# Set-up of a fused FFT and expert layer on one core: unit sums, weight pieces and the order of the early parts

## The chip, the core and the metric

The kernel runs on one NeuronCore of a Trainium2 chip. The core has five engines with queues of their own, each strictly in order: TensorE (PE, its weight loads as PEld), VectorE (DVE), ScalarE (ACT), GpSimd (POOL) and SyncE (SP), which here only starts DMA transfers. TensorE writes to PSUM, the others work in SBUF; GpSimd does not reach PSUM. The metric is the time of one execution on the device in microseconds (us); lower is better.

## The reference

For each of 8 batches a sequence of 3072 rows of 256 numbers goes through a two-dimensional Fourier transform, of which the real part stays. Every one of the 24576 rows then goes through one expert layer of width 2048.

```python
X = np.fft.fft(x, axis=1)            # x: 8 x 3072 x 256
X = np.fft.fft(X, axis=2)
t = X.real.astype(np.float32).reshape(8 * 3072, 256)
h = t @ w_in                         # w_in: 256 x 2048, float64 as given
sp = np.where(h > 20.0, h, np.log1p(np.exp(np.minimum(h, 20.0))))
g = h * np.tanh(sp)                  # the Mish function
out = (g @ w_out).astype(np.float32) # w_out: 2048 x 256, float64 as given
```

## The kernel before

**The transform is folded into the layer.** The second transform is multiplied into w_in once, which gives a cosine and a sine matrix `wch` and `wsh`, each with a rest `wcl` and `wsl` (every fp32 number is held as a rounded part and a rest, so that TensorE's faster fp32r form can be used three times for one exact product). The first transform is a fold (sums and differences of rows on DVE and POOL) followed by matmuls with a table `dft`. A batch gives three chunks of 1024 output rows, held as 512 columns.

**Steps.** The main loop runs over 384 steps: 8 batches x 3 chunks x 16 slices f of the hidden width. Step tau does, in this order: `mm1(tau)`, six matmuls of 512 columns into two PSUM tiles `pa` and `pb` (two buffers of each); `mm2(tau-6)`, twelve matmuls into four accumulators; `make_h(tau)`, three DVE operations from PSUM into a place of the ring `hring`; `split(tau-4)`, in which ACT rounds that step's values to `gh` and POOL computes the rest `gl`; ACT's Mish on the new place; and then whatever is due in the set-up or in the fold of the next batch. `gh` and `gl` have two buffers each, and `hring` has RH = 9 places of 1024 columns, so that make_h(tau) takes the place of step tau-9.

**Set-up.** The weights arrive as float64 bit patterns, in pieces: eight of w_in (two make one quarter of the matrices, which serves four slices f) and eight of w_out (each serves two slices). `load_w` fetches a piece, `conv` turns it into fp32 in three parts: part 0 two DVE bit operations, part 1 two ACT operations, part 2 two DVE operations and a multiply, which is on DVE or POOL as its last argument says (L526). `make_wc` does the matmuls of a quarter, `make_wl` (DVE, L555 and L556) its rests, `split_out` rounds a piece of w_out on ACT (L561) and computes its rest `wol` on POOL (L562). For batch 0, `add_n1` sums the three parts of a unit of x with an identity matrix on TensorE (L676), `fold_z` folds the sums, and `chunk0` gives the first chunk; the sums of the other two chunks follow in `pairs0` and `sums0`, half on DVE (tiles e), half on POOL (tiles o). `other_chunks` makes chunk 1 from them. `col_z`, `col_cs` and `col_out` make the rows of column 0, in 8 partitions.

**What sets the order.** The schedule is written by hand. The table EARLY names a step, a part and its arguments; -1 is before the loop, and within a step the parts are issued in the table's order. OTHER0_AT holds the steps of other_chunks for batch 0, FOLD_AT the steps at which the fold of the next batch begins. `room` says where a piece of weights lives: the first four pieces of w_in in the ring `hring`, the first of w_out in the buffers of gh and gl, the rest in the places of x.

Of the kernel before, what the change touches and what calls it, by code (L numbers as in the profile page):

```python
# [132 lines left out]
OTHER0_AT = (6, 7, 8, 10)  # L133

XPLACES = [('out', 1), ('in', 4), ('in', 5), ('out', 2), ('out', 3), ('in', 6), ('in', 7), ('out', 4), ('out', 5), ('out', 6), ('out', 7)]
EARLY = [
    (-1, 'make_mids', ()),
# [23 lines left out]
    (0, 'conv', ('in', 2, 0)),  # L161
    (0, 'conv', ('in', 3, 0)),
    (0, 'conv', ('in', 2, 1)),
    (0, 'conv', ('in', 3, 1)),
    (0, 'pairs0', (0,)),
    (1, 'conv', ('in', 2, 2, "V")),
    (1, 'conv', ('in', 3, 2, "V")),
    (1, 'sums0', (0, 0, 3)),
    (2, 'make_wc', (1, 0)),
    (2, 'sums0', (0, 3, 7)),  # L170
    (2, 'conv', ('out', 0, 0)),
    (2, 'conv', ('out', 0, 1)),
    (2, 'make_wl', (1,)),
# [4 lines left out]
    (2, 'load_w', ('in', 5)),
    (2, 'load_w', ('out', 2)),
    (3, 'conv', ('out', 0, 2, "V")),  # L180
    (3, 'split_out', (0,)),
    (3, 'sums0', (1, 0, 3)),
    (3, 'col_z', (0,)),
    (3, 'col_z', (1,)),
    (4, 'sums0', (1, 3, 7)),
    (4, 'put_mids', ()),
    (4, 'col_cs', (0,)),
    (4, 'conv', ('in', 4, 0)),
# [3 lines left out]
    (5, 'col_cs', (1,)),
    (5, 'conv', ('in', 4, 2, "V")),
    (5, 'conv', ('in', 5, 2, "V")),
    (5, 'conv', ('out', 1, 0)),
    (5, 'conv', ('out', 1, 1)),
# [704 lines left out]
```

## Time and profile before

| | |
|---|---|
| median of 3 runs (lowest to highest) | 1792.13 us (1790.42 to 1794.56) |
| the profiled execution, its own time | 1792.64 us |
| its span, first to last instruction | 1790.9 us |
| mean granted TensorE clock | 0.984 of full speed |
| busy over the span: PE, PEld | 1738.2 us (97%), 1415.2 us (79%) |
| busy over the span: DVE, ACT, POOL | 1091.0 us (61%), 866.1 us (48%), 1158.5 us (65%) |

Times in rows are microseconds from the span's first instruction. The profile's page gives the whole span in 40 slices of some 45 us: TensorE's busy share is 6, 6, 8 and 8 tenths in the first four of them and 9 from the fifth on. So the rows below look at the first 210 us, and at a few places later for comparison.

### The profile page before, as it was taken

What the parts mean: (1) busy time and instruction counts of PE and PEld (TensorE: products, weight loads), DVE (VectorE), ACT (ScalarE), POOL (GpSimd) and SP (SyncE); (2) the same over time, 40 slices, a digit from 0 to 9 for tenths busy, and PEclk for the clock granted to TensorE, in tenths of its full rate; (3) what the DMA queues carried; (4) which work ended last, traced back from release to release, by engine and by line L of the source; (5) the groups of instructions that cost most, each with busy time, mean ns of one, the idle gap of its engine ahead of it and who ended that gap; (6) DMA issues with size and microseconds to landing.
All of it is one profiled execution on the core that took longest, in us unless ns stands there. A gap on an engine that the chain in (4) does not pass through costs nothing.

```text
span 1790.9 us, 20402 instructions
## 1 busy us (share of the span) xinstructions
PE 1738.2 (97%) x7564; PEld 1415.2 (79%) x7564; DVE 1091.0 (61%) x1635; ACT 866.1 (48%) x968; POOL 1158.5 (65%) x618
## 2 busy tenths in 40 slices
PE   6688899999999999999999999999999999999999
PEld 3356688888888888888888888888888888888887
DVE  3996676556655656556655666556565566554453
ACT  1354454455544545445544555445454555444454
POOL 0536686577765877568765777568765787555455
PEclk8799999999999999999999999999999999998999
DMA  4111200200002000110002000020002000000000
GB/s 164 48 55 52 82 1 30 101 1 30 30 1 100 30 0 30 57 44 30 30 1 100 8 23 30 1 100 30 0 30 100 1 30 30 1 30 1 30 24 24
DMA packets 25158, 67.70 MB, mean 38 GB/s; under 512 B 3043, under 2 KB 3402, under 8 KB 24930
## 3 DMA queue, kind: packets, MB, share of 16 engines
q1 hardware_dynamic: 24354, 64.86, 9.9%
q10 hardware_dynamic: 704, 1.54, 0.2%
q8 instruction: 59, 0.97, 0.2%
q14 instruction: 41, 0.34, 0.1%
HBM read 41.14 MB, written 25.25 MB: 37 GB/s over the span
## 4 chain that ended last, share of the span: by engine, by line
PE 93%; DVE 4%; DMA 1%; POOL 1%; ACT 0%; issue 0%; SPq 0%; DVEq 0%; ACTq 0%
PE acc L755 58%; PE pa L725 5%; PE pa L726 5%; PE pa L727 5%; PE pb L725 5%; PE pb L727 5%; PE pb L726 5%; PE pa L390 2%; PE pb L390 2%; POOL gl L745 0%; DVE woutu L524 0%; DVE hring L735 0%; DVE hring L736 0%; DMA xring<-x_dram 0%; PE pu L676 0%
## 5 line engine op out<-in xcount | busy, mean ns | idle before, releaser
L745 POOL TENSOR_TENSOR gl<-hring,gh 128x1024 fp32r<-128x1024 f32 x384 | 927.2, 2415 | 537.5 <-ACT gh L744 523.9
L744 ACT CAST gh<-hring 128x1024 fp32r<-128x1024 f32 x384 | 403.2, 1050 | 762.5 <-PE acc L755 758.0
L755 PE MATMUL acc<-gh,wol 128*128 128x512 f32 x1536 | 600.5, 391 | 7.8 <-POOL wol L562 7.8
L755 PE MATMUL acc<-gh,woh 128*128 128x512 f32 x1536 | 600.3, 391 | 4.1 <-ACT woh L561 4.1
L734 DVE SCALAR_TENSOR_TENSOR hring<-p0b,wc,pa 128x512 f32<-128x512 f32 x384 | 286.7, 747 | 475.3 <-PE pa L727 455.2
L755 PE MATMUL acc<-gl,woh 128*128 128x512 f32 x1536 | 424.6, 391 | 0.0
L843 ACT ACTIVATE hring<-hring 128x1024 f32<-128x1024 f32 x384 | 404.2, 1053 | 25.1 <-DVE hring L736 25.1
L755 PEld LDWEIGHTS acc<-gh,wol 128*128 128x128 f32 x1536 | 289.6, 189 | 69.4 <-POOL wol L562 9.0
L755 PEld LDWEIGHTS acc<-gh,woh 128*128 128x128 f32 x1536 | 289.4, 188 | 66.0 <-ACT woh L561 5.8
L755 PEld LDWEIGHTS acc<-gl,woh 128*128 128x128 f32 x1536 | 290.2, 189 | 60.7
L735 DVE TENSOR_TENSOR hring<-hring,pb 128x512 f32<-128x512 f32 x384 | 264.0, 688 | 41.7 <-DVE hring L734 1.4
L736 DVE TENSOR_TENSOR hring<-hring,pb 128x512 f32<-128x512 f32 x384 | 263.8, 687 | 13.3
L725 PE MATMUL pa<-ph,wch 128*128 128x512 f32 x384 | 160.2, 417 | 4.3 <-ACT pe L610 3.3
L725 PE MATMUL pb<-qh,wsh 128*128 128x512 f32 x384 | 150.5, 392 | 0.9 <-DVE hring L736 0.9
L726 PE MATMUL pa<-pl,wch 128*128 128x512 f32 x384 | 150.6, 392 | 0.3 <-DVE pl L406 0.3
L727 PE MATMUL pa<-ph,wcl 128*128 128x512 f32 x384 | 150.4, 392 | 0.0
L727 PE MATMUL pb<-qh,wsl 128*128 128x512 f32 x384 | 150.0, 391 | 0.0
L726 PE MATMUL pb<-ql,wsh 128*128 128x512 f32 x384 | 149.9, 390 | 0.0
L725 PEld LDWEIGHTS pa<-ph,wch 128*128 128x128 f32 x384 | 72.8, 190 | 21.3 <-ACT pe L610 3.8
L315 POOL TENSOR_TENSOR o<-xring 128x768 f32<-128x768 f32 x32 | 59.8, 1872 | 44.0 <-DVE F1o L688 43.9
L725 PEld LDWEIGHTS pb<-qh,wsh 128*128 128x128 f32 x384 | 72.6, 189 | 17.0 <-DVE hring L736 1.8
L727 PEld LDWEIGHTS pa<-ph,wcl 128*128 128x128 f32 x384 | 72.6, 189 | 15.5
(205 smaller groups left out, 1125.4 us busy)
## 6 DMA issues: line engine op xcount, KB each, us to landing
xring<-x_dram SPq DMA_DIRECT2D x32, 768.0 KB
out_dram<-ot SPq DMA_DIRECT2D x96, 256.0 KB
p0b<-p_d SPq DMA_DIRECT2D x23, 256.0 KB
xring<-w_out_dram SPq DMA_DIRECT2D x7, 512.0 KB
hring<-w_in_dram SPq DMA_DIRECT2D x4, 512.0 KB
xring<-w_in_dram SPq DMA_DIRECT2D x4, 512.0 KB
dft<-table_dft_dram ACTq DMA_DIRECT2D x1, 1028.0 KB
wraw<-w_out_dram SPq DMA_DIRECT2D x1, 512.0 KB
```

Of the source, the lines that this page charges most:

```text
L315: eng.tensor_tensor(st[c, y, 0][:, w], r[:, :, 0], r[:, :, 1], op=ALU.add if y == "e" else ALU.subtract)
L390: T.matmul(dst, lhs(c), const(c, par, sine), **{"start": c == 0, "stop": c == last, **kw})
L725: T.matmul(dst, wh[:, fs], q[n + "h"], start=True, stop=False)
L726: T.matmul(dst, wh[:, fs], q[n + "l"], start=False, stop=False)
L727: T.matmul(dst, wl[:, fs], q[n + "h"], start=False, stop=True)
L734: V.scalar_tensor_tensor(h[:, 0:512], p0b[ch], wc0[:, f:f + 1], pa, op0=ALU.mult, op1=ALU.add)
L735: V.tensor_tensor(h[:, 512:1024], h[:, 0:512], pb, op=ALU.add)
L736: V.tensor_tensor(h[:, 0:512], h[:, 0:512], pb, op=ALU.subtract)
L744: A.copy(gh, h)
L745: G.tensor_tensor(gl, h, gh, op=ALU.subtract)
L755: T.matmul(acc[i], w[:, f, 128 * d:128 * d + 128], g[:, 512 * t:512 * t + 512], **kw)
L843: A.activation(hring[:, tau % RH], hring[:, tau % RH], AF.Mish)
```

## The change

The diff, cut to the code and to two lines of the table. The new table has 94 rows before its tail where the old one had 91; what its order does is shown below the diff.

```diff
-RH = 9
-FOLD_AT = (20, 10, 44)
+RH = 6
+FOLD_AT = (16, 10, 44)
-OTHER0_AT = (6, 7, 8, 10)
+OTHER0_AT = (11, 12, 13, 14)
-XPLACES = [('out', 1), ('in', 4), ('in', 5), ('out', 2), ('out', 3), ...]
+WPLACES = [('in', 0), ('in', 1), ('out', 0), ('out', 1), ('in', 4), ('in', 5), ('out', 2), ('in', 6), ('in', 7)] + [
+    ('out', i) for i in range(3, NF // 2)]
 EARLY = [
+    (-1, 'warm', (3,)),
...
+    (10, 'sums0', (1, 0, 3)),
...
 ] + [(t, g, a) for i in range(4, NF // 2) for t, g, a in (
-    (2 * i + 4, 'conv', ('out', i, 0)),
-    (2 * i + 4, 'conv', ('out', i, 1)),
-    (2 * i + 5, 'conv', ('out', i, 2, "V")),
-    (2 * i + 5, 'split_out', (i,)),
-)]
+    (2 * i + 3, 'conv', ('out', i, 0)),
+    (2 * i + 3, 'conv', ('out', i, 1)),
+    (2 * i + 4, 'conv', ('out', i, 2)),
+    (2 * i + 4, 'split_out', (i,)),
+    (2 * i + 4, 'load_w', ('out', i + 2)),
+)[:5 if i + 2 < NF // 2 else 4]]
...
+    wring = cp.tile([128, 2, 6 * D], F32, name="wring")
...
     def room(kind, i):
-        if kind == "in" and i < 4:
-            q, k = divmod(i, 2)
-            r = [hring[:, 4 * q + j] for j in range(4)]
-            return r[k], r[2][:, 512 * k:512 * k + 512], r[3][:, 512 * k:512 * k + 512]
-        if kind == "out" and i == 0:
+        if kind == "in" and i in (2, 3):
             tu = gp.tile([128, 1024], F32, tag="gl", name="wtu")
             return gp.tile([128, 1024], F32, tag="gh", name="wraw"), tu[:, :512], tu[:, 512:]
-        r = xring[:, XPLACES.index((kind, i)) % 4]
-        return r[:, :1024], r[:, 1024:], otp.tile([128, 512], F32, tag="ot", name="woutu")
+        r = wring[:, WPLACES.index((kind, i)) % 2]
+        return r[:, :1024], r[:, 1024:], otp.tile([128, 512], F32, tag="ot", name="wu")
...
-    load_w("out", 0)
...
-    def add_n1(c, w):
+    def add_n1(c, w, eng):
         u = 2 * c + w
-        pu = ps(("pa", "pb")[w]) if c == 0 else psacc.tile([128, 512], F32, tag=f"acc{2 + w}", name="pu")
...
+        x = [xring[:, u, 512 * n1:512 * n1 + 512] for n1 in range(3)]
+        if eng == "T":
+            pu = ps(("pa", "pb")[w])
...
+        else:
+            t = fp.tile([128, 512], F32, tag="full1", name="sum")
+            V.tensor_tensor(t, x[0], x[1], op=ALU.add)
+            V.tensor_tensor(t, t, x[2], op=ALU.add)
+            V.tensor_tensor(su, t[:, 0:256], t[:, 256:512], op=ALU.add)
+            V.tensor_tensor(sv, t[:, 0:256], t[:, 256:512], op=ALU.subtract)
+
+    zero = fp.tile([128, 512], F32, tag="full0", name="zero")
+    G.memset(zero, 0.0)
+
+    def warm(n):
+        pz = psacc.tile([128, 512], F32, tag="acc3", name="warm")
+        for _ in range(n):
+            T.matmul(pz, zero[:, :128], zero, start=True, stop=True)
...
-    def pairs0(c):
-        for w in range(2):
-            for y, eng in (("e", V), ("o", G)):
-                pair(0, c, w, y, eng)
+    def pairs0(c, w):
+        for y, eng in (("e", V), ("o", G)):
+            pair(0, c, w, y, eng)
```

With the old table every conv of part 2 in the diff and in the kernel names "V", DVE; in the new one only the first four pieces of w_in do, and the other twelve multiplies are on POOL. The parts pairs0 and sums0 stood in steps 0 to 4 and stand in steps 5 to 10 now; split_out of a w_out piece stands two steps ahead of the first mm2 that uses it, where it stood one step ahead.

TensorE before the loop, in the kernel before (`pw` are the matmuls of w_in's first quarter, `p_213` the first chunk's row):

```order
L576 MATMUL pb<-mids,hring 24x128
L577 MATMUL pb<-mids,hring 1x128
L584 MATMUL pc<-hring,mids 128x16
L585 MATMUL pc<-hring,mids 128x8
L676 MATMUL pa<-xring,hring 128x512 x3
L543 MATMUL pw<-hring,cs 128x512 x4
L676 MATMUL pb<-xring,hring 128x512 x3
L550 MATMUL pw<-ones,hring 128x1 x8
L676 MATMUL pu<-xring,hring 128x512 x3
L639 MATMUL p_213<-dft,hring 128x256 x4
```

The same stretch of TensorE now (three more matmuls on `zero` stand at the very start of the queue):

```order
L578 MATMUL pb<-mids,hring 24x128
L579 MATMUL pb<-mids,hring 1x128
L586 MATMUL pc<-hring,mids 128x16
L587 MATMUL pc<-hring,mids 128x8
L699 MATMUL warm<-zero 128x512 x3
L680 MATMUL pa<-xring,hring 128x512 x3
L680 MATMUL pb<-xring,hring 128x512 x3
L545 MATMUL pw<-wring,cs 128x512 x4
L552 MATMUL pw<-ones,wring 128x1 x8
L641 MATMUL p_224<-dft,hring 128x256 x4
```

The sums of two units stand together, ahead of the first quarter's matmuls, and those of the other two units have left TensorE.

POOL from the split of step 0 to that of step 3, in the kernel before (`wol` is the rest of a w_out piece, `o` and `F1o` are POOL's half of the fold):

```order
L745 TENSOR_TENSOR gl<-hring,gh 128x1024
L325 TENSOR_SCALAR o<-o 128x2x128
L326 TENSOR_TENSOR o<-o 128x2x128
L335 TENSOR_TENSOR o<-o 128x2x128
L344 TENSOR_TENSOR F1o<-o 128x256 x2
L745 TENSOR_TENSOR gl<-hring,gh 128x1024 x2
L562 TENSOR_TENSOR wol<-xring,woh 128x512
L406 TENSOR_TENSOR pl<-spare,ph 128x256
L745 TENSOR_TENSOR gl<-hring,gh 128x1024
```

POOL from the split of step 4 to that of step 6 now (L528 is the multiply of a piece of weights, L321 the pairs):

```order
L762 TENSOR_TENSOR gl<-hring,gh 128x1024
L564 TENSOR_TENSOR wol<-wring,woh 128x512
L331 TENSOR_SCALAR o<-o 128x2x128
L332 TENSOR_TENSOR o<-o 128x2x128
L341 TENSOR_TENSOR o<-o 128x2x128
L350 TENSOR_TENSOR F0o<-o 128x256 x2
L762 TENSOR_TENSOR gl<-hring,gh 128x1024
L528 TENSOR_TENSOR wring<-wring,wu 128x512
L321 TENSOR_TENSOR o<-xring 128x768
L528 TENSOR_TENSOR wring<-wring,wu 128x512
L762 TENSOR_TENSOR gl<-hring,gh 128x1024
```

Before, the first half of the fold was done before the first split and the second half ended right behind it; now both halves stand between the splits of steps 1 to 7, together with the multiplies.

POOL around the splits of steps 12 to 14 now, where the last two pieces of w_out and the next batch's first pair fall:

```order
L762 TENSOR_TENSOR gl<-hring,gh 128x1024 x2
L528 TENSOR_TENSOR wring<-wring,wu 128x512
L564 TENSOR_TENSOR wol<-wring,woh 128x512
L762 TENSOR_TENSOR gl<-hring,gh 128x1024
L412 TENSOR_TENSOR pl<-full_779,ph 128x512
L321 TENSOR_TENSOR o<-xring 128x768
L762 TENSOR_TENSOR gl<-hring,gh 128x1024
L528 TENSOR_TENSOR wring<-wring,wu 128x512
L564 TENSOR_TENSOR wol<-wring,woh 128x512
L412 TENSOR_TENSOR ql<-full_780,qh 128x512
```

Each `wol` has its multiply right ahead of it on the same queue now, and the pair L321 has come in front of the last piece.

## Rows read from the trace of the kernel before

**Rows 1.** Windows: busy time (instructions) of each engine by stage; granted clock, DMA.

```profile
0.00:46.45 46.45, 32.00 (x89) 16.64 (x89) 16.92 (x49) 8.80 (x21) 2.30 (x6) 0.89 0.40 158
46.45:138.49 92.04, 69.93 (x260) 43.44 (x259) 82.89 (x126) 39.44 (x63) 40.50 (x32) 0.87 0.19 67
138.49:205.50 67.01, 55.13 (x208) 42.73 (x207) 42.06 (x58) 30.64 (x39) 38.55 (x21) 0.90 0.17 59
205.50:1790.90 1585.40, 1581.15 (x7014) 1312.43 (x7012) 949.09 (x1405) 787.23 (x846) 1077.15 (x563) 1.00 0.09 32
```

**Rows 2.** Timeline, TensorE before the loop: start, duration, operation, [idle before it, releaser].

```profile
11.78 4.45 PE L676 MATMUL pa<-xring,hring 128*128 128x512 f32 x6 [3.56 <-DMA xring<-x_dram]
...
19.58 6.61 PE L543 MATMUL pw<-hring,cs 128*128 128x512 f32 x8 [3.35 <-issue]
...
43.26 0.70 PE L390 MATMUL pa<-dft,F1e 128*128 128x258 f32 x2 [1.17 <-DVE F1e L688]
...
46.45 0.50 PE L725 MATMUL pa<-ph,wch 128*128 128x512 f32 x1
```

**Rows 3.** Timeline, DVE: the first piece's part 2 behind the first unit's sum.

```profile
17.47 0.68 DVE L524 SCALAR_TENSOR_TENSOR hring<-hring 128x512 int32<-128x512 int32 x1
```

**Rows 4.** Timeline, TensorE: the second quarter of w_in in step 2.

```profile
61.70 4.00 PE L543 MATMUL pa<-hring,cs 128*128 128x512 f32 x4 [10.32 <-DVE hring L526]
```

**Rows 5.** Timeline, DVE and POOL side by side.

```profile
48.85 0.69 DVE L735 TENSOR_TENSOR hring<-hring,pb 128x512 f32<-128x512 f32 x1
48.93 1.30 POOL L332 TENSOR_TENSOR o<-o 128x512 f32<-128x512 f32 x1
...
91.13 2.48 POOL L745 TENSOR_TENSOR gl<-hring,gh 128x1024 fp32r<-128x1024 f32 x1 [3.50 <-ACT gh L744]
91.27 2.89 DVE L525 SCALAR_TENSOR_TENSOR xring<-xring 128x512 f32<-128x512 uint32 x1
```

**Rows 6.** Groups on POOL, 0 to 215 us: busy us, mean ns | idle before, releasers.

```profile
L745 POOL TENSOR_TENSOR gl<-hring,gh 128x1024 fp32r<-128x1024 f32 x20 | 50.1, 2509 | 39.0 <-ACT gh L744 26.1 <-PE acc L755 12.9
L315 POOL TENSOR_TENSOR o<-xring 128x768 f32<-128x768 f32 x5 | 9.7, 1954 | 44.0 <-DVE F1o L688 43.9
L562 POOL TENSOR_TENSOR wol<-xring,woh 128x512 fp32r<-128x512 f32 x7 | 9.6, 1366 | 6.5 <-ACT woh L561 6.5
```

**Rows 7.** Timeline, DVE: conversion of pieces while POOL is idle.

```profile
95.41 0.68 DVE L525 SCALAR_TENSOR_TENSOR xring<-xring 128x512 f32<-128x512 uint32 x1
96.12 0.69 DVE L526 TENSOR_TENSOR xring<-xring,woutu 128x512 f32<-128x512 f32 x1
96.73 0.42 DVE L518 TENSOR_SCALAR woutu<-xring 128x512 int32<-128x512 int32 x1
97.07 0.42 DVE L519 TENSOR_SCALAR xring<-xring 128x512 int32<-128x512 int32 x1
```

**Rows 8.** Timeline, TensorE: waits for w_out's pieces.

```profile
155.68 0.79 PE L755 MATMUL acc<-gh,wol 128*128 128x512 f32 x1 [2.31 <-POOL wol L562]
...
194.15 0.49 PE L755 MATMUL acc<-gh,woh 128*128 128x512 f32 x1 [2.91 <-ACT woh L561]
```

**Rows 9.** Timeline, DVE: first operation of make_h in steps 11, 22, 34 and 35.

```profile
139.60 0.74 DVE L734 SCALAR_TENSOR_TENSOR hring<-p0b,wc,pa 128x512 f32<-128x512 f32 x1
...
205.51 0.74 DVE L734 SCALAR_TENSOR_TENSOR hring<-p0b,wc,pa 128x512 f32<-128x512 f32 x1
...
253.75 0.75 DVE L734 SCALAR_TENSOR_TENSOR hring<-p0b,wc,pa 128x512 f32<-128x512 f32 x1 [0.95 <-PE pa L727]
...
257.83 0.75 DVE L734 SCALAR_TENSOR_TENSOR hring<-p0b,wc,pa 128x512 f32<-128x512 f32 x1 [1.82 <-PE pa L727]
```

**Rows 10.** Windows, matmuls of line 390 alone: one call of other_chunks.

```profile
101.83:103.67 1.84, 1.84 (x8) 1.43 (x8) 1.00 0.00 0
```

**Rows 11.** Timeline: POOL's splits of steps 111 and 112, make_h of step 117.

```profile
610.47 4.97 POOL L745 TENSOR_TENSOR gl<-hring,gh 128x1024 fp32r<-128x1024 f32 x2
613.42 0.75 DVE L734 SCALAR_TENSOR_TENSOR hring<-p0b,wc,pa 128x512 f32<-128x512 f32 x1 [0.26 <-PE pa L727]
```

More of the change, by code (lines that the diff above doesn't have):

```diff
@@ L160 @@
     (-1, 'chunk0', (1, 2)),
[L161 to L173, printed above, removed]
+    (-1, 'conv', ('in', 2, 0)),
+    (-1, 'conv', ('in', 3, 0)),
@@ L174 @@
+    (-1, 'conv', ('in', 2, 1)),
+    (-1, 'conv', ('in', 3, 1)),
+    (0, 'conv', ('in', 2, 2, "V")),
+    (0, 'conv', ('in', 3, 2, "V")),
+    (0, 'conv', ('out', 0, 0)),
+    (0, 'conv', ('out', 0, 1)),
+    (1, 'make_wc', (1, 0)),
+    (1, 'col_z', (0,)),
+    (1, 'col_z', (1,)),
+    (1, 'conv', ('out', 0, 2)),
+    (1, 'conv', ('out', 1, 0)),
+    (1, 'conv', ('out', 1, 1)),
+    (1, 'make_wl', (1,)),
     (2, 'make_wc', (1, 1)),
-    (2, 'pairs0', (1,)),
-    (2, 'load_w', ('out', 1)),
+    (2, 'col_cs', (0,)),
@@ L177 @@
+    (2, 'split_out', (0,)),
     (2, 'load_w', ('in', 4)),
[L178 to L188, printed above, removed]
+    (2, 'conv', ('out', 1, 2)),
+    (3, 'col_cs', (1,)),
+    (3, 'split_out', (1,)),
+    (3, 'load_w', ('in', 5)),
@@ L189 @@
+    (3, 'conv', ('in', 4, 0)),
+    (3, 'conv', ('in', 4, 1)),
+    (3, 'col_out', (1,)),
     (4, 'conv', ('in', 5, 0)),
-    (4, 'conv', ('in', 4, 1)),
     (4, 'conv', ('in', 5, 1)),
[L192 to L196, printed above, removed]
+    (4, 'conv', ('in', 4, 2)),
+    (4, 'col_out', (2,)),
+    (5, 'conv', ('in', 5, 2)),
+    (5, 'pairs0', (0, 0)),
     (6, 'make_wc', (2, 0)),
-    (6, 'conv', ('out', 1, 2, "V")),
@@ L212 @@
+    (7, 'sums0', (0, 0, 3)),
+    (8, 'split_out', (2,)),
+    (8, 'load_w', ('in', 7)),
     (8, 'conv', ('in', 6, 0)),
     (8, 'conv', ('in', 6, 1)),
+    (8, 'sums0', (0, 3, 7)),
     (9, 'conv', ('in', 7, 0)),
     (9, 'conv', ('in', 7, 1)),
[L216 to L219 removed]
+    (9, 'conv', ('in', 6, 2)),
+    (9, 'pairs0', (1, 0)),
+    (9, 'conv', ('in', 7, 2)),
     (10, 'make_wc', (3, 0)),
[L221 removed]
+    (10, 'make_wc', (3, 1)),
@@ new lines @@
+    (10, 'conv', ('out', 3, 0)),
+    (10, 'conv', ('out', 3, 1)),
+    (10, 'sums0', (1, 3, 7)),
+    (10, 'put_mids', ()),
+    (10, 'conv', ('out', 3, 2)),
+    (11, 'load_w', ('out', 4)),
+    (11, 'split_out', (3,)),
+    (11, 'load_w', ('out', 5)),
+] + [(t, g, a) for i in range(4, NF // 2) for t, g, a in (
+    (2 * i + 3, 'conv', ('out', i, 0)),
[4 more added lines that the diff above has]
+)[:5 if i + 2 < NF // 2 else 4]]
@@ L670, in fft_moe @@
     folds[0] = {}
-    def add_n1(c, w):
+    def add_n1(c, w, eng):
         u = 2 * c + w
-        pu = ps(("pa", "pb")[w]) if c == 0 else psacc.tile([128, 512], F32, tag=f"acc{2 + w}", name="pu")
-        for n1 in range(3):
-            T.matmul(pu, eye, xring[:, u, 512 * n1:512 * n1 + 512], start=n1 == 0, stop=n1 == 2)
-        plus, minus = pu[:, 0:256], pu[:, 256:512]
         su, sv = (uv[:, i, w].rearrange("p h j -> p (h j)") for i in range(2))
-        A.copy(sv, minus)
-        V.tensor_tensor(su, plus, sv, op=ALU.add)
-        V.tensor_tensor(sv, plus, sv, op=ALU.subtract)
+        x = [xring[:, u, 512 * n1:512 * n1 + 512] for n1 in range(3)]
+        if eng == "T":
+            pu = ps(("pa", "pb")[w])
+            for n1 in range(3):
+                T.matmul(pu, eye, x[n1], start=n1 == 0, stop=n1 == 2)
+            plus, minus = pu[:, 0:256], pu[:, 256:512]
+            A.copy(sv, minus)
+            V.tensor_tensor(su, plus, sv, op=ALU.add)
+            V.tensor_tensor(sv, plus, sv, op=ALU.subtract)
+        else:
[10 more added lines that the diff above has]
+            T.matmul(pz, zero[:, :128], zero, start=True, stop=True)
     def fold_z(c):
```

47 lines of the change are left out of this document (18 added, 29 removed).

## The prediction

> **What bounds the kernel now.** I read the windows by stage first [rows 1]. From 205.5 us on TensorE is busy 1581.15 of 1585.40 us at full clock, so only the first 205 us can give anything. They split into three stages. Before the loop (to 46.45 us) TensorE is busy 32 us and waits for data. In steps 0 to 10 (46.45 to 138.49) DVE is busy 82.9 of 92.0 us and TensorE 69.9, at a granted clock of 0.87. In steps 11 to 21 (to 205.5) neither DVE nor POOL is full; TensorE is busy 55.1 of 67.0 us, and clock 0.90 says that part of that is slow too. A step of the loop at full clock takes 4.08 us, from one make_h to the next [rows 9], so eleven steps need 44.9 us.
>
> The timelines then give the reason in each stage. Before the loop TensorE's first real matmuls wait for x until 11.78 us and take 4.45 us at half clock; the first quarter of w_in begins at 19.58 us, after 3.35 us of idleness, because its conversion on DVE stands behind the first unit's sum [rows 2, 3]. In step 2 TensorE stands 10.32 us until DVE has converted the next quarter [rows 4]. In the third stage it waits for the halves of w_out's pieces in four places; of the first the wait for `wol` stands in the rows, 2.31 us, of the last that for `woh`, 2.91 us [rows 8].
>
> One more thing is to be seen, since the change moves work between DVE and POOL: the two do not run side by side. DVE's L525 starts at 91.27, just behind POOL's gl, and takes 2.89 us, to 94.16, where it takes 0.68 with POOL idle; it ends 0.55 us after gl does (91.13 + 2.48 = 93.61) [rows 5, 7]. L735 takes its plain 0.69 us during a POOL operation; its second input lies in PSUM [rows 5]. So a DVE operation that works in SBUF alone waits for POOL's running one, and the times of both engines add up, except for make_h, the rests of w_in and the chunks' combinations.
>
> **Part 1, before the loop.** The conversion of two pieces now stands ahead of the unit sums on DVE. Part 2 is 0.68 + 0.68 + 0.69 = 2.05 us a piece [rows 7]; before, it began at 17.47 us [rows 3] and two pieces were ready at some 21.5. Now it only follows ACT's part 1, which I put at 10 to 11 us (the mids, ahead of it on ACT, wait about 0.5 us behind three matmuls on zeros), so both are ready at about 14.3. TensorE sums units 0 and 1 from 11.8 to about 17 (half of 4.45 us each at full clock, the second behind its data), then the quarter, 3.3 us at full clock instead of 6.61 [rows 2]. The zeros are to bring that clock: TensorE is busy almost from 1 us on. DVE now ends last: folds of units 0 and 1 at 20.2, then units 2 and 3 at 2 x 0.69 and two of half the width, estimated 2.2 us each, the rests of the quarter 1.4, the last folds 1.8: 27.8 us. From the matmul on F1e to the loop are 46.45 - 43.26 = 3.2 us [rows 2]; F1e is ready 0.9 us before the folds end, so mm1(0) stands at about 30.5, 16 us earlier. If the clock isn't raised, TensorE's chain ends last and it is about 37.
>
> **Part 2, steps 0 to 10.** I walk the steps with the rows' durations. Steps 0 to 3: DVE converts w_in 2 and 3 (2 x 2.05) and TensorE waits about 5 us for it instead of 10.32 [rows 4]; make_h(1) ends at 42, make_h(2) at 49, and POOL's first split starts at about 59 us. Pairs and sums of batch 0, which filled this time before, come later.
>
> In steps 4 to 10 the two engines' SBUF work is, on POOL by mean durations [rows 6]: 7 splits x 2.51 = 17.6, six multiplies of pieces x 1.37 (the shape of wol) = 8.2, one wol 1.4, four pairs x 1.95 = 7.8, and the sums, an estimate from L332's 1.30 us for 512 columns [rows 5] and half of that for 256, 12.4; together 47.4. On DVE [rows 7]: ten bit operations x 0.42 = 4.2, twelve operations of part 2 x 0.68 = 8.2, four pairs at about 1.0 (one and a half widths of L526), sums about 6, column 0 0.7; together 23. The sum is 70.4 us, against 5 x 4.08 + 2 x 1.4 + 10.5 (two quarters), some 34 us, on TensorE. So here the pair of engines is the bound: step 10 is through at 59 + 70.4 = 129 if neither ever waits for anything else. The whole stage before had 10 conversions x 2.89 + 11 us on DVE and 40.5 on POOL [rows 1], 80.7 in 92.0 us, or 88%; at that share it would be 139. The walk gives 128 for make_h(11); TensorE stands for some 8 and 16 us around the quarters in steps 6 and 10 and comes back at half clock, as it did at 61.70 (4.00 us for two matmuls) [rows 4], for which I add 4. I take 132, against 139.60 [rows 9]: 7.6 us. Of the 16 us of lead, half is lost here, because the same sums meet the splits and the multiplies in one queue.
>
> **Part 3, steps 11 to 21.** Before: 205.51 - 139.60 = 65.9 us [rows 9]. Now 44.9 us of steps, plus four calls of other_chunks x 1.8 [rows 10], 7.2 (before, three of the four lay ahead of step 11). The pieces of w_out come a step earlier, but their multiply and wol stand behind the split on POOL: split 2.4 + multiply 1.37 + ACT 0.6 + wol 1.37 after gh, 6.7 us from the end of a step's mm2. In steps 12 and 14, which are 5.9 us long, that is in time; the piece of step 16 is about 1 us late, that of step 18 about 4, since a pair and the last chunk's rests come in front of it. 44.9 + 7.2 + 5 = 57, a gain of 9.
>
> **Parts that cost nothing here.** A ring of 6 makes make_h(117) wait for the split of step 111, which ends at about 612.96, 0.46 us before make_h(117) starts at 613.42 [rows 11]; that is the closest of the 378 pairs in the trace, the median is 2.1 us, so it is hidden, and even if one came late make_h has the second PSUM buffer as cover. In steps 11 to 13, where splits run late, it could bind; that is within the 4 us above. The next batch's x no longer waits for weight pieces, a wait nobody else sat behind; bounds 0 and 1 us.
>
> **Sum.** 7.6 + 9 = 16.6 us off the profiled execution's 1792.64; that stands 0.5 us above the median, so 1775.5 to 1776: I say 1776.
>
> The Trainium skill (SBUF — State Buffer, section "SBUF: two separate sides") calls the port pair that VectorE and GpSimd share an exclusive lock, held for a whole instruction and taken by a VectorE operation with two SBUF inputs. The rows agree: 2.89 us behind a split, 0.69 with an input in PSUM. By that rule each multiply moved to POOL takes 1.37 us of the pair instead of 0.69, twelve of them 8 us more, and it speaks against the change; without it stage 2 would be rival A.
>
> **Rivals.**
> A. Alternating costs little, as most DVE operations find gaps while POOL waits for gh. Then POOL's 47 us and DVE's own queue bound steps 4 to 10, make_h(11) comes at about 115 to 118, and with part 3 the gain is about 33: 1759. For it: POOL is busy 44% of that stage now [rows 1]. Against: L525's wait. Chance 0.2.
> B. The pair of engines runs at the 88% of before: 139 for make_h(11), no gain; and in part 3 the late pieces eat half of the 9. 1787. Chance 0.16.
> C. Slower: POOL's queue. Between the splits of steps 3 and 7 stand all of the fold's operations and five multiplies; gl comes late, mm2 waits for gl, gh's two buffers wait for mm2, ACT's queue stands behind gh, and with it the conversion of the next piece, so that POOL and DVE wait for ACT in turn. It decides from the point where steps 4 to 10 need more than 89 us (a share under 79%), because then make_h(11) comes later than 148 and part 3's 9 us are gone. At 70% they need 100: 20 us later than before at step 11, 11 in all: 1803. For it: ACT already waits for POOL and TensorE in this stage. Chance 0.12.
> D. The zeros don't raise the clock, or it falls before x is there: 6 us later into the loop, the rest as forecast: 1782. Chance 0.07.
>
> **How the numbers follow.** My forecast has 0.45, with 1769 to 1783 as its own range (129 to 136 for make_h(11), 3 to 8 us of late pieces). About 0.2% (3.6 us) is what a measurement of this kernel can tell from no change. A, D and the forecast are faster; half of B is within 0.2%; C is slower. Faster 0.81, same 0.08, slower 0.11. The range that leaves 2 in 10 out reaches into A and past B: 1757 to 1791.
>
> **What would show it.** mm1(0) at 30 to 31 us, with the unit sums at full clock; POOL's first split near 59; from there to about 130 us POOL and DVE taking turns, DVE's bit operations often over 1 us, and TensorE waiting for the quarters in steps 6 and 10; make_h(11) near 132 and make_h(22) near 189; waits for wol of 1 and 4 us at the last two pieces of w_out only. I am wrong if DVE's SBUF operations keep their plain durations there (A), or if TensorE's wait in steps 7 to 10 is for gl and ACT's queue is what stands behind it (C).

## The result and the profile after

The changed kernel took 1767.35 us (median of 4 runs, 1765.5 to 1770.45) where the kernel before took 1792.89 in the same comparison (1790.42 to 1794.56): a ratio of 0.986, 95% interval 0.9842 to 0.9879, or 25.5 us less. The forecast was 1776 with a range of 1757 to 1791. The sign and the range held; the size was too small by 8.65 us. The profiled execution took 1765.5 us, 1.9 below the median, with a span of 1763.7.

The windows by stage answer to those of before [rows 1]. The columns are the same: length, busy time of PE, PEld, DVE, ACT and POOL, granted clock, DMA share, GB/s. The cuts lie 0.65 us behind the start of mm1(0) (29.45) and at the first operation of make_h in steps 11 and 22; the second cut of before, 138.49, lies 1.11 us ahead of make_h(11).

```profile
0.00:30.10 30.10, 28.09 (x91) 15.16 (x92) 19.29 (x56) 8.43 (x20) 0.73 (x5) 1.00 0.67 262
30.10:121.23 91.13, 70.00 (x251) 43.10 (x249) 76.00 (x105) 39.27 (x59) 53.08 (x37) 0.83 0.14 41
121.23:181.04 59.81, 52.48 (x211) 41.24 (x211) 48.91 (x67) 30.95 (x42) 48.49 (x28) 0.94 0.25 93
181.04:1763.70 1582.66, 1578.46 (x7016) 1310.78 (x7014) 945.50 (x1403) 787.74 (x846) 1073.02 (x561) 1.00 0.09 32
```

By the starts of mm1(0) and make_h, the loop begins 17.0 us earlier (46.45 - 29.45), stage 2 takes 91.8 us where it took 93.2, and stage 3 is 6.1 us shorter. The first stage was to be led by conversions that stand ahead of the sums, and by zeros that raise the clock. The timeline of TensorE before the loop shows both, beside [rows 2]:

```profile
1.31 5.49 PE L699 MATMUL warm<-zero 128*128 128x512 f32 x6 [1.31 <-POOL zero L693]
...
8.43 2.84 PE L699 MATMUL warm<-zero 128*128 128x512 f32 x6
11.65 2.84 PE L680 MATMUL pa<-xring,hring 128*128 128x512 f32 x6 [0.38 <-DMA xring<-x_dram]
14.33 2.74 PE L680 MATMUL pb<-xring,hring 128*128 128x512 f32 x6
16.91 3.60 PE L545 MATMUL pw<-wring,cs 128*128 128x512 f32 x8
...
29.45 0.50 PE L742 MATMUL pa<-ph,wch 128*128 128x512 f32 x1
```

The first three matmuls on zeros take 5.49 us, twice the 2.74 of the second unit's sum, which has the same form; so they ran at half clock and the sums at full clock. The first unit's sum takes 2.84 us where it took 4.45, the quarter of w_in 3.60 where it took 6.61, and it follows the sums without a gap.

From there I compare the first operation of make_h, step by step, in the two timelines of DVE ([rows 9] has those of steps 11 and 22 before):

| step | 0 | 4 | 7 | 11 | 14 | 17 | 20 | 22 | 23 to 356 |
|---|---|---|---|---|---|---|---|---|---|
| before, us | 48.00 | 79.10 | 105.95 | 139.60 | 151.91 | 173.53 | 193.37 | 205.51 | |
| after, us | 31.64 | 56.13 | 77.24 | 121.23 | 139.78 | 154.01 | 168.54 | 181.04 | |
| lead, us | 16.4 | 23.0 | 28.7 | 18.4 | 12.1 | 19.5 | 24.8 | 24.5 | 23.9 |

The lead grows by 6.6 us in steps 0 to 3 (the second quarter is waited for 3.35 us where it was 10.32) and to 28.7 in step 7. It falls to 12.1 in step 14, in the steps that hold the sums now (5 to 10) and the four calls of other_chunks (11 to 14), and comes back at w_out's last pieces. In the loop after that nothing moves. The last 3.3 us of this execution's 27.1 come at its end and belong to the clock, as told further down. Without them the lead is 23.9; the medians differ by 25.5, and the changed kernel's runs alone spread over 5 us.

That DVE and POOL block each other is to be seen in stage 2, as in [rows 5]. The timeline, with the split of step 0 on POOL between two operations of DVE:

```profile
58.29 0.42 DVE L520 TENSOR_SCALAR wu<-wring 128x512 int32<-128x512 int32 x1
58.34 2.62 POOL L762 TENSOR_TENSOR gl<-hring,gh 128x1024 fp32r<-128x1024 f32 x1 [0.69 <-ACT gh L761]
58.63 2.63 DVE L521 TENSOR_SCALAR wring<-wring 128x512 int32<-128x512 int32 x1
```

A bit operation, 0.42 us long in the first row, takes 2.63 behind the split. TensorE's longest wait in this stage is for POOL's multiply of a piece of the last quarter:

```profile
102.82 2.08 PE L545 MATMUL pa<-wring,cs 128*128 128x512 f32 x2 [7.32 <-POOL wring L528]
106.92 2.07 PE L545 MATMUL pa<-wring,cs 128*128 128x512 f32 x2 [2.02 <-POOL wring L528]
```

In stage 3 its waits for w_out's halves are half of what they were. The view of waits of TensorE (total us, times, longest), before from 138 to 206 us and then after from 120 to 190:

```profile
PE acc L755 <- POOL wol L562: 7.8, 4, 2.3
PE acc L755 <- ACT woh L561: 4.1, 4, 2.9
```

```profile
PE acc L772 <- ACT woh L563: 3.0, 2, 2.3
PE acc L772 <- POOL wol L564: 2.7, 3, 1.0
```

Together they fall from 11.9 to 5.7 us. Only pieces 4 to 7 are split a step earlier than before; split_out of piece 3 has moved from step 10 to step 11, and 1.54 of the 5.7 us are waits for that piece.

### The profile page after: what moved, and what is told of

Read it like the earlier page. It is cut to its first block, busy times and chain, and to the rows that moved or that the text cites. A ratio compares the mean times of both kernels' runs of the same rounds, so it can differ in the third digit from the quotient of the medians.

```text
span 1763.7 us, 20454 instructions
## 1 busy us (share of the span) xinstructions
PE 1729.0 (98%) x7564; PEld 1410.3 (80%) x7564; DVE 1089.7 (62%) x1627; ACT 866.4 (49%) x966; POOL 1175.3 (67%) x631
## 3 DMA queue, kind: packets, MB, share of 16 engines
q10 hardware_dynamic: 704, 1.54, 0.2%
## 4 chain that ended last, share of the span: by engine, by line
PE 93%; POOL 3%; DVE 3%; DMA 1%; issue 1%; ACT 0%; POOLq 0%; DVEq 0%; ACTq 0%
PE acc L772 58%; PE pa L742 5%; PE pa L743 5%; PE pb L744 5%; PE pb L743 5%; PE pb L742 5%; PE pa L744 5%; PE pa L396 2%; PE pb L396 2%; POOL gl L762 1%; POOL wring L528 1%; DMA xring<-x_dram 0%; POOL wol L564 0%; DVE wring L521 0%; PE pb L545 0%
## 5 line engine op out<-in xcount | busy, mean ns | idle before, releaser
L772 PEld LDWEIGHTS acc<-gl,woh 128*128 128x128 f32 x1536 | 289.1, 188 | 60.2 <-POOL gl L762 0.2
L743 PEld LDWEIGHTS pb<-ql,wsh 128*128 128x128 f32 x384 | 72.4, 189 | 16.1 <-POOL ql L412 0.9
```

The lines of the kernel that those rows point to most:

```text
L743: T.matmul(dst, wh[:, fs], q[n + "l"], start=False, stop=False)
L772: T.matmul(acc[i], w[:, f, 128 * d:128 * d + 128], g[:, 512 * t:512 * t + 512], **kw)
```

## The experiments

Each run changes the changed kernel in one respect, e9 to e11 in two or three. "Later" and "earlier" compare make_h with the changed kernel's at the same step. Medians are of 4 or 5 runs; the changed kernel's is 1767.35. Where the interval of a ratio reaches into the changed kernel's, 0.9842 to 0.9879, the times alone don't separate the two: that is so for e1, e2, e5, e6, e7, e8, e9 and e10, and there the step times have to speak.

### e1: without the six matmuls on zeros

```diff
-    (-1, 'warm', (3,)),
...
-    (-1, 'warm', (3,)),
```

> The changed kernel (1767.35 us) without its six matmuls on zeros. My theory: the sums of units 0 and 1 then run at half clock (4.45 us each as in the kernel before, not 2.84 and 2.74), the quarter behind them partly too, and mm1(0) comes 4 to 7 us later (29.45 in the changed kernel's profile, then 34 to 37); DVE, which ends last there, follows TensorE's sums, and all later steps move with it: 1772 to 1774. Rival: the steps 4 to 10, where DVE and POOL take turns, have room for the delay, and it is gone by step 11: 1767 to 1769.

1770.78 us (1770.61 to 1772.12), ratio to the kernel before 0.9881 (0.9868 to 0.9895). TensorE's sums before the loop:

```profile
11.75 4.83 PE L678 MATMUL pa<-xring,hring 128*128 128x512 f32 x6 [3.50 <-DMA xring<-x_dram]
16.41 2.74 PE L678 MATMUL pb<-xring,hring 128*128 128x512 f32 x6
...
18.99 3.60 PE L543 MATMUL pw<-wring,cs 128*128 128x512 f32 x8
```

Only the first sum is slow, and not all of it (5.49 would be half clock throughout); the second and the quarter are at full clock. mm1(0) comes 2.1 us later, less than the 4 to 7 of the theory; 1.9 to 2.4 stay through step 20 and 3.4 from step 21, so the rival is refuted. What adds the last 1.2 us at step 21 is open; e12 has them there too. The zeros are worth 2 us where they act, and the medians differ by 3.4. Rival D had put 6 us on them.

### e12: the first quarter's conversion behind the unit sums again

```diff
-    (-1, 'conv', ('in', 0, 2, "V")),
-    (-1, 'conv', ('in', 1, 2, "V")),
...
     (-1, 'add_n1', (0, 1, 'T')),
+    (-1, 'conv', ('in', 0, 2, "V")),
+    (-1, 'conv', ('in', 1, 2, "V")),
```

> The conversion of w_in's first two pieces (six DVE operations, 3.95 us) stands behind the sums of units 0 and 1 on DVE again, as in the kernel before; all else as changed. Theory: in the changed kernel these operations lie in time that DVE spends waiting (9.28 to 13.2 us, ahead of the first sum's result at 14.94); put behind they come on top, the quarter's matmuls start at about 22.4 instead of 16.91, and mm1(0) is 4 us later, at about 33.5; 4 us stay to the end, 1771. Rival 1: the quarter sets the start, and at half clock after 5 us of idleness; mm1(0) 6 to 8 us later, 1774. Rival 2: a later start is given back where POOL and DVE are full in steps 4 to 10, as half of the lead was forecast to be: 2 us or less at make_h(11), 1768 to 1769.

In this order w_out's first two pieces are fetched into the places of w_in's first two before those are converted, so the first quarter is computed from other values, and the conversion waits for that transfer too. 1776.43 us (1775.11 to 1779.19), ratio 0.9908 (0.9895 to 0.9922). DVE, then TensorE:

```profile
17.97 0.42 DVE L684 TENSOR_TENSOR uv<-pb,uv 128x256 f32<-128x256 f32 x1
21.20 0.69 DVE L526 SCALAR_TENSOR_TENSOR wu<-wring,wu 128x512 int32<-128x512 int32 x1 [2.80 <-DMA wring<-w_out_dram]
...
23.32 6.60 PE L545 MATMUL pw<-wring,cs 128*128 128x512 f32 x8 [6.25 <-issue]
```

mm1(0) is 8.8 us later. Of that, 2.80 is the wait for the transfer, which this edit brought in by itself; the quarter at half clock after 6.25 us of idleness (6.60 instead of 3.60) is rival 1's mechanism, and the conversion's 3.95 us on DVE now lie on the path. The two can't be told apart with this run, so its size is not a clean test of 4 against 6 to 8. Rival 2 is refuted cleanly: 8.8 us at step 0 are 8.8 at step 11 and 9.8 from step 21 on (6.9 in step 13 alone). A later start is not given back.

### e3: all four units' sums on TensorE

```diff
+    (-1, 'add_n1', (1, 0, 'T')),
+    (-1, 'add_n1', (1, 1, 'T')),
...
-    (-1, 'add_n1', (1, 0, 'V')),
...
-    (-1, 'add_n1', (1, 1, 'V')),
...
-            pu = ps(("pa", "pb")[w])
+            pu = ps(("pa", "pb")[w]) if c == 0 else psacc.tile([128, 512], F32, tag=f"acc{2 + w}", name="pu")
```

> The changed kernel with the sums of units 2 and 3 on TensorE as before the change, right behind the first quarter's matmuls, into two accumulators. My theory: TensorE does 2 x 2.6 us more before the first chunk's matmuls and DVE 2 x 1.4 us less; TensorE then ends last, mm1(0) comes about 3 us later than 29.45, and the run takes 1769 to 1771. Rival: DVE was the one that ended last, so taking 2.8 us off it brings mm1(0) forward: 1764 to 1766.

1775.83 us (1772.38 to 1777.23), ratio 0.9905 (0.9891 to 0.9918). TensorE:

```profile
22.65 5.42 PE L680 MATMUL pu<-xring,hring 128*128 128x512 f32 x12 [0.25 <-ACT wc L553]
29.49 1.96 PE L641 MATMUL p<-dft,hring 128*128 128x256 f32 x8 [1.43 <-issue]
```

The sums of units 2 and 3 take 5.42 us on the path of the first chunk, and mm1(0) stands at 36.3 us, 6.9 later; 5.9 are left at step 11 and 7.5 from step 21. Sharing the sums out is worth more than I had expected, the rival is refuted, and one us is given back by step 11.

### e2 and e5: multiplies back on DVE

e2 moves all twelve multiplies of pieces to DVE, e5 only the four of w_in's pieces 4 to 7, on which TensorE's 7.32 us wait ends. The edit is the same in each place:

```diff
-    (4, 'conv', ('in', 4, 2)),
+    (4, 'conv', ('in', 4, 2, "V")),
```

> The changed kernel with all sixteen multiplies of the pieces on DVE, as before, and nothing else moved. My theory (a DVE operation in SBUF and a POOL operation exclude each other): a multiply takes 0.69 us of the pair instead of 1.3, so twelve of them free 7 us of it, and TensorE's waits for POOL's multiplies at the quarters (12.4 us in all) get shorter; DVE's own queue is 12 x 0.61 = 7 us longer. Between the two: 1761 to 1767, not slower. Rival (the queues are independent, and taking work off DVE is what gained): 7 us more on DVE in steps 1 to 18, 1771 to 1775.

e2: 1773.68 us, ratio 0.9877 (0.9857 to 0.9896); the five runs are 1766.22, 1767.23, 1773.68, 1773.82 and 1774.18. The profiled one is the last. TensorE's waits from 60 to 130 us in it:

```profile
PE pa L545 <- DVE wring L528: 12.9, 3, 7.2
PE pa L545 <- DVE hring L751: 4.5, 1, 4.5
PE pa L742 <- DVE hring L751: 1.5, 1, 1.5
```

The wait for the multiply is as long as it was (12.4 us, three times, longest 7.3, in the changed kernel), now behind DVE's queue instead of POOL's, and make_h itself comes late: 8.1 us at step 11, 5.4 from step 22. But the granted clock from 58.34 to 121.23 us was 0.73 in this execution and 0.81 in the changed kernel's, and two of the five runs are no longer than the changed kernel. The two short runs fit the theory's 1761 to 1767, the three long ones the rival's 1771 to 1775, and neither is decided: the multiplies on POOL gain something between nothing and 7 us, and no run shows that they cost anything.

> The changed kernel with the multiplies of w_in's pieces 4 to 7 on DVE, w_out's eight still on POOL. TensorE's waits for POOL's multiply at the quarters are 12.4 us in the changed kernel. Theory 1 (DVE's own queue sets steps 4 to 10, as the run with all multiplies on DVE showed, 8 us later at make_h(11)): four multiplies are 2.4 us more on that queue, and TensorE only waits for DVE instead; make_h(11) 1 to 4 us later, 1768 to 1771. Theory 2 (POOL's queue makes the pieces late, and the pair's time decides): the quarters come 1.5 to 3 us earlier, 1763 to 1766.

e5: 1769.3 us (1766.33 to 1773.82), ratio 0.9872 (0.9852 to 0.9892), in two pairs of runs, 1766.4 and 1772 to 1774; 0.9 us later at step 11, 0.8 from step 23 in the profile of a run of the first pair. Equal, within what can be told here. The quarters' waits are not shortened by taking their multiplies off POOL: they are 15.0 us in this profile, now for DVE, against 12.4. So theory 2 is not borne out; whether theory 1's 1 to 4 us are lost is within the spread.

### e4: w_out's pieces 4 to 7 one step later

```diff
-    (2 * i + 3, 'conv', ('out', i, 0)),
-    (2 * i + 3, 'conv', ('out', i, 1)),
-    (2 * i + 4, 'conv', ('out', i, 2)),
-    (2 * i + 4, 'split_out', (i,)),
-    (2 * i + 4, 'load_w', ('out', i + 2)),
+    (2 * i + 4, 'conv', ('out', i, 0)),
+    (2 * i + 4, 'conv', ('out', i, 1)),
+    (2 * i + 5, 'conv', ('out', i, 2)),
+    (2 * i + 5, 'split_out', (i,)),
+    (2 * i + 5, 'load_w', ('out', i + 2)),
```

> The changed kernel with the w_out pieces 4 to 7 converted and split one step later, as in the kernel before (multiply still on POOL). My theory: TensorE waits for wol at the first mm2 of each piece, and since the multiply now stands ahead of wol on POOL the wait is longer than the 2.7 us of before: 4 pieces x 2.5 to 4 us, 1775 to 1782, with all of it between make_h(11) and make_h(22). Rival: that stage is bound by DVE and POOL taking turns, their work is the same, and the waits only move: 1766 to 1770.

1784.99 us (1782.66 to 1787.93), ratio 0.996 (0.9947 to 0.9972). Waits of TensorE from 100 to 200 us:

```profile
PE acc L772 <- ACT woh L563: 12.6, 5, 4.0
...
PE acc L772 <- POOL wol L564: 3.9, 5, 0.8
```

make_h is 4 us earlier at steps 12 and 13, then 8.2 later at step 17 and 16.3 from step 21. The theory's place is right, its size too small, and the waits are for `woh` more than for `wol`; the rival is refuted. Of the 16.3 us, 10.8 are longer waits for w_out's halves (16.5 against 5.7). Most of the rest is slower matmuls: between make_h(11) and make_h(22) the same 211 matmuls keep TensorE busy 59.2 us, at a granted clock of 0.87, where they took 52.5 at 0.94. This is the largest loss from a single part put back, 17.6 us in the time. But e4 is not the order of before: there the multiply stood on DVE, and the waits were 11.9 us and not 16.5. How much of the 17.6 us comes from the late step with the multiply on DVE was not tried.

### e6: a ring of 5 places

```diff
-RH = 6
+RH = 5
```

> The changed kernel with a ring of 5 places instead of 6 (nothing else; no reason but to measure the ring). make_h of a step then waits for the split of the step five before, which ended 2.1 us (median) ahead of make_h with six and so would end about 2 us after it with five. My theory: the second PSUM buffer covers make_h being 2 to 3 us late in every step, so steady steps stay at 4.08 us: 1767 to 1771, with 1 to 3 us lost where splits run late in steps 7 to 18. Rival: the chain make_h, Mish, split four steps later, make_h closes on itself and every step gets longer: 1.5 us x 370, about 2300.

1772.55 us (1771.2 to 1773.7), ratio 0.9881 (0.9866 to 0.9896). DVE's waits from 30 to 200 us, and the windows of the steady loop:

```profile
DVE hring L751 <- POOL gl L762: 9.6, 5, 4.8
```

```profile
200.00:1640.00 1440.00, 1439.38 (x6361) 1192.01 (x6360) 1019.86 (x1307) 741.37 (x777) 1022.82 (x523) 1.00 0.09 32
```

All 5.3 us are lost by step 22, where the theory had 1 to 3. In the steady loop make_h waits for the split 172 times from 200 to 1640 us, 315 us in all, and TensorE doesn't notice: busy 1439.38 of 1440 us. So the rival's 2300 is refuted, and since the steady loop loses nothing even with one place fewer, the ring of 6 costs nothing there. Ahead of it the ring of 6 binds once: make_h(20) of the changed kernel waits 1.92 us for a split. What a ring of 9 would give in that step was not tried.

### e7 and e8: the next batch's fold, and the third quarter

e7 lets the fold of batch 1 begin in step 20 again. e8 makes the third quarter of w_in in step 7 at once, with its rests later there, and the fourth quarter's rests behind the sums in step 10.

```diff
-FOLD_AT = (16, 10, 44)
+FOLD_AT = (20, 10, 44)
```

> The changed kernel with the fold of the second batch begun at step 20, as before the change, instead of 16. Theory: in the changed kernel the last two pieces of w_out are late, and the pair in front of the last one makes it so (TensorE waits 2.3 us for woh and 1.5 for wol at most); without the pair the last piece is on time, make_h(22) comes 2 to 4 us earlier: 1763 to 1765. Rival: the pair is then done at step 20 to 22 at the same price, or ACT's order makes the piece late: 1766 to 1768.

e7: 1765.02 us (1764.09 to 1765.17), ratio 0.9838 (0.9824 to 0.9853). 3.5 us earlier from step 21 in the profile; the pair of the next batch (2.29 us on POOL) no longer stands in front of w_out's last piece. The theory is borne out in the steps: make_h(22) comes 3.0 us earlier, and the longest wait for `woh` is 0.8 us where it was 2.3. All four runs lie below the four of the changed kernel, though the profiled ones differ by 0.3 us only, since e7's loses 3 us near its end, as told further down.

```diff
-    (6, 'make_wc', (2, 0)),
-    (6, 'make_wl', (2,)),
...
+    (7, 'make_wc', (2, 0)),
...
+    (7, 'sums0', (0, 0, 3)),
+    (7, 'make_wl', (2,)),
...
-    (7, 'sums0', (0, 0, 3)),
...
-    (10, 'make_wl', (3,)),
...
+    (10, 'make_wl', (3,)),
```

> The changed kernel with the third quarter of w_in made a step later (step 7 instead of 6, its rests behind three of the fold's operations) and the rests of the fourth behind three of the fold's operations in step 10. In the changed kernel DVE stands 1.74 + 2.72 us in step 6 and 1.95 + 1.55 in step 10 until ACT has copied the quarter, and TensorE stands for the pieces. Theory: DVE's in-order queue sets steps 4 to 10, so its waits of 8 us are what can be had: make_h(11) 4 to 8 us earlier, 1759 to 1764. Rival: the pair DVE and POOL is full there and the waits only move: 1766 to 1769.

e8: 1767.78 us (1762.39 to 1768.6), ratio 0.9848 (0.9833 to 0.9864). 4.5 us earlier at step 7, 2.1 at step 11, 3.0 at step 14; then 3 us later at step 19 and 0.7 earlier from step 21. The theory holds in direction at step 11 (2.1 us of its 4 to 8), and the time is the rival's. The lead is lost where w_out's last pieces come: TensorE waits 4.6 us for `woh` in stage 3, against 3.0.

### e9, e10, e11: the two together, and w_out's last pieces a step earlier still

e9 has the edits of e7 and e8. e10 has that of e7 and this one; e11 has all three:

```diff
-    (2 * i + 3, 'conv', ('out', i, 0)),
-    (2 * i + 3, 'conv', ('out', i, 1)),
-    (2 * i + 4, 'conv', ('out', i, 2)),
-    (2 * i + 4, 'split_out', (i,)),
-    (2 * i + 4, 'load_w', ('out', i + 2)),
+    (2 * i + 3 - (i > 4), 'conv', ('out', i, 0)),
+    (2 * i + 3 - (i > 4), 'conv', ('out', i, 1)),
+    (2 * i + 4 - (i > 4), 'conv', ('out', i, 2)),
+    (2 * i + 4 - (i > 4), 'split_out', (i,)),
+    (2 * i + 4 - (i > 4), 'load_w', ('out', i + 2)),
```

> FOLD_AT 20 and the third quarter made in step 7 with its rests later, together. Theory: the lead of the early quarter is lost at the last pieces of w_out, because the next batch's first pair stands in front of them on POOL; with the fold four steps later that queue is short, and the two gains add: make_h(22) 5 to 6.5 us earlier than in the changed kernel, time about 1762. Rival: the last pieces are late by their own multiply and rest behind a split on POOL, whatever the fold does, and any lead above some 3.5 us is lost there again: make_h(22) 3 to 4 us earlier, 1764.5 to 1765.5.

e9: 1766.05 us, ratio 0.9848 (0.9835 to 0.9862), from two pairs of runs: 1763.33 and 1763.49, 1768.61 and 1768.63. The profiled run is one of the long pair, and its trace shows where the 5 us are, in steps 2 and 3, which e7, e8 and e9 share instruction for instruction. From 42 to 58 us the granted clock is 1.00 in e8's profile and 0.62 in e9's. Two rows of TensorE's timeline in that stretch, first in e8:

```profile
47.27 1.84 PE L552 MATMUL pa<-ones,wtu 128*128 128x1 f32 x16
49.04 1.04 PE L396 MATMUL pa<-dft,hring 128*8 128x258 f32 x4
```

and then in e9:

```profile
47.52 3.41 PE L552 MATMUL pa<-ones,wtu 128*128 128x1 f32 x16
50.86 1.89 PE L396 MATMUL pa<-dft,hring 128*8 128x258 f32 x4
```

The same matmuls, of one column in the first row and into eight partitions in the second, run at half clock in e9. make_h(3) is 5.2 us later for it. At step 22 e9 is 0.4 us later than the changed kernel, so 4.8 earlier without that, if the 5.2 us pass through as the delays of e1 and e12 did. That fits the theory's lower end (5 to 6.5) better than the rival's 3 to 4, and its two undisturbed runs, 1763.4, lie between the two forecasts. I don't call it decided.

> FOLD_AT 20, and w_out's pieces 5 to 7 converted and split one step earlier still. Theory: TensorE's waits for woh and wol in steps 11 to 21 (4.8 us with FOLD_AT 20) go, as they did by 16 us from the step that the change itself took them ahead: make_h(22) 2 to 4 us earlier than with FOLD_AT 20 alone, time about 1762. Rival: two steps are enough; one step more puts multiplies and rests in front of splits and the chunks' rests on POOL, gl comes later, and nothing is gained: within 1 us of FOLD_AT 20 alone, 1764.5 to 1766.

e10: 1765.04 us (1764.74 to 1767.23), ratio 0.9845 (0.9832 to 0.9859), the same as e7's 1765.02. The rival is right. Waits of TensorE from 119 to 185 us:

```profile
PE acc L772 <- POOL gl L762: 2.0, 2, 1.4
PE acc L772 <- POOL wol L564: 0.9, 1, 0.9
...
PE acc L772 <- ACT woh L563: 0.6, 1, 0.6
```

The waits for `woh` and `wol`, 4.8 us with e7's edit alone, are down to 1.5; 2.0 us of waits for `gl` have come in their place, and make_h is 5.8 us later at step 18 and 1.7 earlier at step 21. What a piece gains in POOL's queue, a split loses there.

> FOLD_AT 20, the third quarter in step 7, and w_out's pieces 5 to 7 one step earlier. If the late pieces are what eats the lead: 7 to 9 us ahead of the changed kernel at make_h(22), time about 1759. If POOL's sum of work in steps 11 to 17 is what eats it (splits, rests and multiplies one after the other, wherever they stand): 3.5 to 4.5 us ahead, 1764 to 1765.

e11: 1761.68 us (1761.02 to 1763.61), ratio 0.9826 (0.9812 to 0.9839), whose interval ends below that of the changed kernel (0.9842 to 0.9879). It is the fastest of all, 5.7 us under the changed kernel, though 2.7 short of the 1759 of its first theory: 2.8 us earlier at step 22, 3.5 from step 23, with 1.5 us lost to the clock in step 2 in the profiled run. With those 1.5 us put back, step 22 is 4.3 us ahead, as the second theory had it (3.5 to 4.5); the median lies between the two theories. So POOL's sum of work fits the steps, and the time leaves it undecided.

## Why the prediction was right, and where its sizes were not

**The start: right, with two prices off.** mm1(0) was to come at about 30.5 and came at 29.45; the sums ran at full clock behind the zeros, and POOL's first split was to start "at about 59" and did at 58.34. Two prices were misread. "4.45 us at half clock" was half clock in part only, so that the sums took 2.84 and 2.74 us and not half of 4.45; and without the zeros mm1(0) was to come at about 37, where e1 has 31.5, since there only the first sum is slow. e1, e3 and e12 show that each piece carries its share: without the zeros 2.1 us at step 0, with the sums on TensorE 6.9, and with the old order 8.8 (2.80 of them the added transfer).

**Steps 4 to 10: the mechanism is seen, the size failed.** The step that failed is "The sum is 70.4 us", with the "I add 4" behind it. It put the end of step 10 at 129, the walk at 128, and the forecast at 132; it came at 121.23. The first split before, the window from the first split to step 11 now, and then two groups of POOL in it (busy us, mean ns | idle before them, releasers):

```profile
81.27 2.35 POOL L745 TENSOR_TENSOR gl<-hring,gh 128x1024 fp32r<-128x1024 f32 x1
```

```profile
58.34:121.23 62.89, 45.62 (x161) 30.54 (x161) 52.58 (x66) 23.20 (x31) 47.97 (x33) 0.81 0.14 43
```

```profile
L762 POOL TENSOR_TENSOR gl<-hring,gh 128x1024 fp32r<-128x1024 f32 x7 | 17.0, 2423 | 5.2 <-ACT gh L761 5.2
L528 POOL TENSOR_TENSOR wring<-wring,wu 128x512 f32<-128x512 f32 x5 | 7.7, 1549 | 7.2 <-DVE wring L527 7.2
```

The 62.89 us can be counted up from the timelines of POOL and DVE. POOL was busy 47.97 us, as forecast (47.4). In 11.4 of the other 14.9 us DVE ran an operation other than make_h and the rests of w_in, and in 3.5 neither did. So the pair was in use for 59.4 us, 94% of the stage, and did bound it; what failed is adding all of DVE's 23 us to POOL's 47.4, where 11.4 came on top. The same count gives 59.5 us in e1, e3 and e12, whose first splits start at 60.43, 64.48 and 67.19, and their stages take 62.7 to 63.0 us: a delay at the start goes through this stage unchanged.

Why about half of DVE's time lies inside POOL's is settled in part only. POOL's recorded times hold time in which DVE blocked it: a split that takes 2.34 us at its shortest in this stage takes up to 2.62, a multiply 1.26 and up to 1.91. And a recorded duration overlaps the next: L526 starts at 61.18 and L527 at 61.79, 0.61 apart, with 0.68 recorded for each. The 41 operations of DVE other than make_h and the rests, with 0.07 each, and 33 of POOL with 0.05 are an estimated 4.5 us. The rest is open.

For the 4 us of the clock there was hardly room: the clock did fall to 0.81, but the 3.5 us in which neither of the pair worked are all that slow matmuls can have added, and no run shows how much of them they did. In e2's profile, at the lower clock, neither worked for 10.5 of the 70.7 us between the first split and step 11, and the pair was in use for 60.2. So of the 22.9 us of lead at the first split (81.27 - 58.34) only 4.5 were lost by step 11, where I had 14.7; "half is lost here" is what the runs refute. (In the price of rival B, 28.9 + 11 + 40.5 is 80.4 and not 80.7, which changes nothing.)

**Steps 11 to 21: right in mechanism, 3 us short.** I put 57 us and it took 59.81, so that the gain was 6.1 and not 9. The late pieces themselves were sized well: 5 us forecast, 5.7 measured, with 0.99 us for the piece split in step 16 and 2.32 + 0.85 for that of step 18, where I had 1 and 4. But 3.0 of the 5.7 are waits for `woh` and not for `wol`, since `woh` too stands behind the multiply on POOL's queue, and 1.54 of the 5.7 fall on piece 3, in step 12. What I had left out are 1.9 us of other waits of TensorE in this stage, most of them for make_h and for `ql`, and 0.4 us of slower matmuls (busy 52.5, where 44.9 + 7.2 is 52.1, at a clock of 0.94).

**The sum.** 18.4 + 6.1 = 24.5 against 7.6 + 9 = 16.6: stage 2 gave 10.8 us more than forecast and stage 3 2.9 less, and part of the nearness of 1776 is that the two errors go against each other. The time lies in the stated range because that was drawn out toward A, not because the forecast's own sum held. The 0.6 between steps 22 and 23 goes off, and the profiled run's last 3.3 us are the clock at the end, where the 48 matmuls of 8 columns of the single rows stand. By groups of operations, one of their three lines in the kernel before, then in the one after:

```profile
L799 PE MATMUL pa<-endl,wch 128*128 128x8 f32 x16 | 5.0, 310 | 0.0
```

```profile
L816 PE MATMUL pa<-endl,wch 128*128 128x8 f32 x16 | 4.1, 258 | 0.0
```

In that stretch the clock fell to 0.74 over 20 us in the kernel before and to 0.75 in e7, but to 0.91 in the changed kernel's profiled run. Since e7, which shares this part of the loop with the changed kernel, loses it too, I put it down to the execution and not to the change.

**The rivals.** A is half right. Its sign against it is there, for DVE's operations do wait behind POOL's, but only half of DVE's time came on top of POOL's: make_h(11) at 121.23 lies 3 us above A's 115 to 118 and 8 us below the forecast's own 129 to 136. Of the times, A's 1759 is as near to 1767.35 as the forecast's 1776, and 1767.35 lies below the forecast's own range of 1769 to 1783. B (139 at step 11) and C (a lost stage 3) are refuted by 121.23 and 59.81; TensorE waited for `gl` up to 210 us only in stage 3 of e10 and e11. D is refuted by the sum's 2.84 us.

**The shared ports.** The Trainium skill (SBUF — State Buffer, section "SBUF: two separate sides") calls the pair of ports that VectorE and GpSimd share an exclusive lock. The row at 58.63 agrees: 2.63 us for an operation of 0.42, which ends 0.30 us after the split that started ahead of it. In the prediction I set 8 us against the multiplies on POOL. e2 measured no such loss: with all of them on DVE the fastest run took 1766.22 us, where the changed kernel's took 1765.5, the median was 6.3 us longer, and in the profiled run the pair was in use no shorter (60.2 us against 59.4 from the first split to step 11). One reason that the trace shows is DVE's queue, which is in order and holds make_h: there make_h came 8.1 us later at step 11. How much of that is the clock is open.

**Not tried.** The place of other_chunks (steps 11 to 14) and of pairs0 and sums0 (steps 5 to 10) was not undone by itself, nor were the places of the pieces in `wring`; their part in the fall of the lead from 28.7 to 12.1 us is read from the table only. A single undone part costs 3.4 (e1), 8.5 (e3), 9.1 (e12) or 17.6 us (e4) in the time, more together than the 25.5 of the whole, so the parts cover each other and are no sum.

## What to carry to other kernels

A lead won at the start was kept here where the later waits for data moved ahead with it: look for the last piece that is waited for and take its conversion ahead. When two engines share a bound, don't add up all recorded durations of both: here that gave 70.4 us for a stage of 62.9. Count in a timeline how much of the second engine's time falls outside the first's, and give a third engine no more than what the two leave free. Whether work moved to a slower engine pays depends on the queue that it leaves; here the runs don't decide it.
